# All sixteen row blocks of mm1 by groups of seven products in one of nine tiles, in an order of its own

## The chip, the cores and the metric

The kernel runs on one core of one Trainium2 chip. Its time is device microseconds (us) of one execution of the program; less is better. The engines of the core are called PE (matrix multiplies; its weight loads are PEld), DVE (vector), ACT (activations and copies), POOL (general) and SP (issues transfers). Each engine works through its own queue in order, and semaphores hold an instruction until what it needs is done.

## The reference

Two parts follow each other. First, attention in chunks of 64 tokens: q, k and v have 8 batches, 8 heads, 576 tokens and 64 features, and every chunk attends to itself alone. Then a layer of two matrix multiplies with an exact GELU between them, over 4608 tokens:

```python
scores = scale * np.matmul(q_c, k_c.transpose(0, 1, 2, 4, 3))   # chunks of 64 tokens
attn = softmax(scores)                                          # with 1e-9 in the divisor
x = np.matmul(attn, v_c)                                        # laid out as 4608 x 512
h = x @ w_in                                                    # 512 x 2048
g = 0.5 * h * (1.0 + erf(h * inv_sqrt2))
out = g @ w_out                                                 # 2048 x 512
```

Inputs and the output are float32; the kernel multiplies in bf16 and adds up in float32.

## The kernel before

**Tiles.** The tokens are worked in nine tiles of 512 (NT = 9, index t from 0 to 8): tile t below 8 holds the first 512 tokens of batch t, tile 8 the last 64 tokens of all eight batches. For each tile there is an attention part, which fills x (512 features by 512 tokens, as four slices of 128 partitions), then mm1 (h, 2048 rows by 512 tokens, as sixteen row blocks of 128), then mm2 (the output, 512 by 512). The attention of tile t + 1 and parts of tile t + 2 are laid between the matmuls of tile t.

**mm1, plain.** mm1_slot (L472) makes one row block by four matmuls of 128 x 128 weights (w_in) against 512 columns of x (L477), which add up in one PSUM bank, and one GELU on ACT (L479) that writes h.

**mm1, by seven.** seven_rows (L560) makes four row blocks at once, as a 2 x 2 block matrix of 256 x 256 pieces with seven block products in place of eight. A product is four matmuls of 256 columns (L575). The price is sums: of w_in blocks (w_in_sums, L552, four subtractions or additions on DVE for each group of four row blocks), of x blocks (x_sums, L558, four for each tile, shared by its groups), and of products. The steps of one group, with the names that the orders use (one, two or three primes mark the group: none is row blocks 0 to 3, ' is 4 to 7, '' is 8 to 11):

```python
"p1": product("a", w(0, 0), x_block(t, 0, 0), True)
"s11": AC(place_of("b"), bank["a"])             # ACT copies a to b
"p5": product("d", ws[0], x_sum(1), True), AC(kept, bank["d"])
"p2": product("b", ...)    "c11": gelu of b     # one quarter of h
"p6": product("a", ...)    "s12": d = a + kept  # DVE, L579
"p4": product("d", ...)    "c12": gelu of d
"p7": product("a", ...)    "c22+": kept = a + kept, "c22": gelu of kept
"p3": product("a", w(1, 1), x_sum(4)), gelu of a
```

So a product that adds into bank a (p6, p7, p3) comes after the step that read a before it: p7 after s12, p3 after c22+. PSUM has eight banks in three pools (AT 3, TP 2, MM 3); banks a, b and d of each group are taken from them as they come free.

**Homes.** The sums of w_in for the first group lie in a part of w_out_sb that is not read any more, those of the second in w_in_more, and those of the third in one of the six staging tiles, which third_home (L541) keeps for good at the loads of tile 5; the kept p5 of the third group lies there too.

**The order.** In the tiles 5 to 8 every step is laid by hand in a tuple (FIFTH, LATER, LAST, chosen by WHOLE, L501). A number in it is a plain row block; p, s and c steps are those above; the rest are hooks that whole_hooks (L979) ties to functions. T0 is quad_totals of the next tile (L284: four additions L290, a reciprocal L291, a first spread rc L300, two more reciprocals L296, all on DVE). R0 to R3 are quad_rc (L300, DVE). AV is quad_av (L334, 64 small matmuls on PE). X0 to X3 are quad_x (L341, DVE, they fill x of the next tile). XS1 to XS4 are x_sums of the next tile. S1 to S4, in halves a and b, are g_sum, the sums of h blocks that mm2 needs (L654, L667, DVE). S is quad_S of the tile after the next, with its exponentials on ACT; P0 to P3 are quad_part, its partial sums on DVE (a transpose L256 and a reduction L259 each); KC0 to KC3 are ACT copies for it. exp and gelu load ACT's function table (L865). Each Y is one of the fourteen stations of mm2: two for each of its seven products, 16 matmuls of 256 columns to a product (L731). Y0 opens mm2; what stands before the first Y0 is mm1.

**Tile 7 before.** It follows LATER: three groups by seven (row blocks 0 to 11), the blocks 12 to 15 plain. It has no tile after the next, so S, P and KC do nothing there (tile 8's were made in tile 6); exp and gelu are still issued.

Of the kernel before, what the change touches and what calls it, by code (L numbers as in the profile page):

```python
# [11 lines left out]
def kernel(  # L12
# [26 lines left out]
    NT = B + 1  # L39
# [176 lines left out]
    AT, TP, MM = (ps_at, "at"), (ps_tp, "tp"), (ps_mm, "mm")  # L216
# [255 lines left out]
    def mm1_slot(t, f):  # L472
# [3 lines left out]
        for ks in range(KS):  # L476
# [5 lines left out]
    T0 = 3  # L482
# [14 lines left out]
    LAST = ("p1", "p5", "s11", 13, 14, "p1'", "s11'", "p2", "c11", "p6", "p1''", "s11''", 15, "p5'", "s12", "p7", "p2''", "c22+",  # L497
# [3 lines left out]
    WHOLE = {T0 + 2: FIFTH, NT - 1: LAST, **{t: LATER for t in range(T0 + 3, NT - 1)}}  # L501

    HF = FF // 2
    HD = d_model // 2
# [33 lines left out]
                [w_in_more[:, i] for i in range(4)]]  # L538
    kept_more = []

    def third_home():  # L541

        raw, n = stage_tile(), 4 * HD
        w_in_sum.append([raw[:, i * HD:(i + 1) * HD].bitcast(bf16).rearrange("p (k n) -> p k n", k=2) for i in range(4)])
        kept_more.append(raw[:, n:n + HM * HD].rearrange("p (m n) -> p m n", m=HM))
# [14 lines left out]
    def seven_rows(t, of, pools, kept, bank):  # L560

        h = tiles[t]["h"]
        w, ws = lambda r, c: w_in_block(r, c, of), w_in_sum[of]

        def place_of(to):
            if to not in bank:
                pool, tag = pools[to]
                bank[to] = pool.tile([P, HM, HD], f32, tag=tag, name="hs_ps")
            return bank[to]

        def product(to, left, right, fresh=False):
            hs = place_of(to)
            for f in range(HM):
                for ks in range(2):
                    nc.tensor.matmul(hs[:, f], left[:, ks, f * P:(f + 1) * P], right[:, ks],  # L575
                                     start=(fresh and f == 0 and ks == 0), stop=(ks == 1), skip_group_check=True)

        def plus(to, src):
            nc.vector.tensor_tensor(to, bank[src][:], kept, op=ADD)  # L579

        def gelu(r, c, src):
            n = HM * (2 * of + r)
            nc.scalar.activation(h[:, n:n + HM, HD * c:HD * (c + 1)], src, Act.Gelu)  # L583

        return {
            "p1": lambda: product("a", w(0, 0), x_block(t, 0, 0), True),
            "p5": lambda: (product("d", ws[0], x_sum(1), True), AC(kept, bank["d"][:])),
            "s11": lambda: AC(place_of("b")[:], bank["a"][:]),
            "p2": lambda: product("b", w(0, 1), x_block(t, 1, 0)),
            "c11": lambda: gelu(0, 0, bank["b"][:]),  # L590
            "p6": lambda: product("a", ws[1], x_sum(2)),
            "s12": lambda: plus(bank["d"][:], "a"),
            "p4": lambda: product("d", ws[3], x_block(t, 1, 1)),
            "c12": lambda: gelu(0, 1, bank["d"][:]),
            "p7": lambda: product("a", ws[2], x_sum(3)),
            "c22+": lambda: plus(kept, "a"),
            "c22": lambda: gelu(1, 1, kept),
            "p3": lambda: (product("a", w(1, 1), x_sum(4)), gelu(1, 0, bank["a"][:]))}

    def mm1_seven(t, hooks):  # L600

        if t > 1:
            tiles[t]["h"] = hpool.tile([P, FF, MT], bf16, tag="h", name="h")
        kept = [work.tile([P, HM, HD], f32, tag="t1", name="kept_p5", bufs=2)[:] for _ in range(2 if t in TWICE else 1)]
        bank, more, third = {}, {}, {}
        if t == 1:
            does = seven_rows(t, 1, {"a": TP, "b": AT, "d": AT}, kept[0], bank)
        else:
            does = seven_rows(t, 0, {"a": AT, "b": AT, "d": AT}, kept[0], bank)
        if t in TWICE:  # L610
            does.update((step + "'", do) for step, do in
                        seven_rows(t, 1, {"a": TP, "b": TP, "d": AT}, kept[1], more).items())
            if t not in WHOLE:
                fifth = does["p5'"]
                does["p5'"] = lambda: (more.update(d=bank["b"]), fifth())
        if t in THRICE:
            pools = dict.fromkeys("abd", MM) if t == NT - 1 else {"a": MM, "b": AT, "d": AT}
            does.update((step + "''", do) for step, do in seven_rows(t, 2, pools, kept_more[0], third).items())
        if t in WHOLE:
            order = WHOLE[t][:WHOLE[t].index("Y0")]  # L620
        elif t == T0 + 1:
            order = (4, 5, 6, "p1", "s11", 7, "p2", "p5", "c11", "p6", 8, "s12", "t0", 9, 10, "p4", "p7", "c12", "c22+",
                     "t1", 11, "c22", 12, "p3", "g0", 13, "s3", 14, 15)
        elif t == T0:
            order = ("p1'", "s11'", "x", "p1", "s11", 8, 10, "k", "p6'", "p2", "c11", 11, "p6", "p5", "p5'", "p2'", "c11'", 9, 13,
                     "s12", "p7", "s12'", "p4", "c22+", "p7'", "c12", "c22", "p4'", "c12'", 15, "p3", "c22+'", "p3'", "c22'", 12,
                     "g0", 14)
        elif t == 2:
            order = ("p1", "s11", "p1'", "x", "s11'", 8, "p2", "c11", "p5", 9, "p6", "s12", "p5'", "p6'", "s12'", 10, "p7", 11,
                     "c22+", "c22", "p7'", 12, "p4", "c12", "p3", "c22+'", "p3'", 13, "p4'", "p2'", "k", "c22'", "c11'", "c12'",  # L630
                     "g0", 14, 15, "s3")
        else:
            order = (9, "p1", "s11", 10, 11, "w", "p5", "p2", "c11", "p6", 12, "s12", "w0", "p4", "p7", "c12", "c22+", "w1", 13,
                     "c22", "p3", 14, "g0", "s3", 15)
        for step in order:
            if step in does:
                does[step]()
                continue
            for u in hooks.get(step, ()):
                u()  # L640
            if not isinstance(step, str):
                mm1_slot(t, step)
# [224 lines left out]
    with tc.manual_schedule():  # L867
# [111 lines left out]
        def whole_hooks(t):  # L979

            n = t + 1
            acts = {f"S{i}{'ab'[a]}": lambda i=i, a=a: g_sum(t, i, a) for i in (1, 2, 4) for a in range(2)}
            acts["S3"] = lambda: g_sum(t, 3)
            if n < NT:
                acts.update(T0=lambda: quad_totals(n), AV=lambda: quad_av(n, ALONE),
                            exp=lambda: act_table(Act.Exp), gelu=lambda: act_table(Act.Gelu))
                for m in range(G):
                    acts[f"R{m}"] = lambda m=m: quad_rc(n, m // 2, m % 2)
                    acts[f"X{m}"] = lambda m=m: quad_x(n, m // 2, m % 2)
                    acts[f"XS{m + 1}"] = lambda m=m: x_sums(n, (m,))  # L990
            if n + 1 < NT:
                acts["S"] = lambda: quad_S(n + 1, ALONE)
                for m in range(G):
                    acts[f"KC{m}"] = lambda m=m: k_by_chunk(n + 1, AC, (m,))
                    acts[f"P{m}"] = lambda m=m: quad_part(n + 1, m // 2, m % 2)
            if t == T0 + 2:
                acts.update(W0=lambda: w_in_sums(2, (0, 1)), W1=lambda: w_in_sums(2, (2, 3)))
            e1, e2, slot = {}, {}, 0
            for step in WHOLE[t]:
                if str(step)[0] == "Y":  # L1000
                    slot += 1
                elif step in acts:
                    if slot:
                        e2.setdefault(slot, []).append(acts[step])
                    else:
                        e1[step] = [acts[step]]
            return e1, e2
# [17 lines left out]
        for t in range(1, NT):  # L1025
# [24 lines left out]
            def next_loads():  # L1050
                if t + 3 == NT - 1:
                    load_qk(t + 3, "k")
                    pool_cast_qk(t + 3, "k")
                elif t + 3 < NT:
                    bring_qk(t + 3)
                if n + 1 < NT:
                    load_v_rows(n + 1)
                    cast_v_rows(n + 1, PO)
                if t + 3 == NT - 1:
                    third_home()  # L1060
            if t == T0:
                flip(n + 1, "q")
            elif t > T0:
# [77 lines left out]
```

## Time and profile before

| what | us |
|---|---|
| median of 3 runs | 270.4 (269.82 to 270.89) |
| the profiled execution | 270.2 |
| its span | 268.4, so 1.8 lie around it |
| PE busy | 259.9 (97%) |
| DVE busy | 215.1 (80%) |
| ACT busy | 199.8 (74%) |
| POOL busy | 91.1 (34%) |
| tile 7: mm1 | 214.13 to 226.75, 12.62 |
| tile 7: mm2 | 226.75 to 239.75, 13.00 |
| tile 8: mm1 | 239.75 to 252.37, 12.62 |

The span runs from the first to the last instruction of the profiled execution, and all positions are us from its start. A group line of the profile gives code line, engine, operation, what is written and read, count, busy time and mean duration. A timeline line gives start, duration, engine, code line, operation, what is written and read, shapes and count; idle time of the engine ahead of it and what ended it stand in brackets. A matmul's duration contains its way through the array, so successive matmuls overlap: their rate is read from their starts.

### The profile page before, as it was taken

The page shows a single profiled execution, that of the slowest core. Times are in us where ns is not written, and L with a number is a line of the kernel's source. Part 1 is how long each engine was busy: PE and PEld are TensorE (multiplying, and loading weights), DVE is VectorE, ACT ScalarE, POOL GpSimd, SP SyncE. Part 2 cuts the span into 40 slices and gives each one's busy share as a digit, 9 for nine tenths or more (in the row PEclk, how much of TensorE's full clock was granted, in tenths as well). Part 3 has the DMA queues.
Part 4 walks back from the last instruction along what each step waited for, and adds up shares of the span by engine and source line. Part 5 has one row for each costly group of instructions (what it writes and reads, how often), then busy time and mean ns, then how long its engine had stood idle before and what let it go on. Part 6 is the DMA issues. An engine that isn't in the chain of part 4 may idle for free.

```text
span 268.4 us, 7377 instructions
## 1 busy us (share of the span) xinstructions
PE 259.9 (97%) x2977; PEld 196.7 (73%) x2977; DVE 215.1 (80%) x362; ACT 199.8 (74%) x384; POOL 91.1 (34%) x150
## 2 busy tenths in 40 slices
PE   7699999999999999999999999999999999999994
PEld 2478775556886788678855887688778877887883
DVE  5874877999995899778998999897899979943753
ACT  3767758888676967799977967987899789448810
POOL 7777769511167111912732910305102100000000
PEclk9999999999999999999999999999999999999999
DMA  6999999899699899999899639998954120121014
GB/s 209 265 334 401 391 404 230 230 236 273 217 383 237 192 192 313 235 285 331 220 228 330 156 96 188 220 138 167 272 117 109 42 81 0 42 83 36 1 42 118
DMA packets 104739, 53.97 MB, mean 201 GB/s; under 512 B 72960, under 2 KB 101632, under 8 KB 104704
## 3 DMA queue, kind: packets, MB, share of 16 engines
q1 hardware_dynamic: 104400, 53.23, 75.2%
q8 instruction: 23, 0.38, 0.6%
q10 hardware_dynamic: 304, 0.26, 0.3%
q14 instruction: 12, 0.10, 0.1%
HBM read 36.70 MB, written 9.44 MB: 172 GB/s over the span
## 4 chain that ended last, share of the span: by engine, by line
PE 70%; SPq 11%; DMA 9%; POOL 4%; ACT 3%; issue 1%; DVE 0%; POOLq 0%
PE y_ps L731 26%; PE hs_ps L575 15%; PE h_ps L477 12%; SPq L128 7%; DMA arrival<-in_k_dram 5%; PE h_ps L451 5%; SPq L194 3%; PE y_ps L801 3%; POOL k_nat L164 2%; DMA arrival<-in_v_dram 2%; DMA k_t<-k_nat 2%; ACT k_bd L188 2%; PE h_ps L467 2%; PE y_ps L765 1%; PE av_ps L334 1%
## 5 line engine op out<-in xcount | busy, mean ns | idle before, releaser
L477 PE MATMUL h_ps<-x,w_in_sb 128*128 128x512 bf16 x220 | 53.8, 379 | 0.0
L479 ACT ACTIVATE h<-h_ps 128x512 bf16<-128x512 f32 x69 | 41.2, 600 | 13.1 <-PE h_ps L477 8.6
L731 PEld LDWEIGHTS <-h 128*128 128x128 bf16 x384 | 37.0, 98 | 4.5
L164 POOL CAST q_nat<-arrival 128x512 bf16<-128x512 f32 x31 | 22.2, 755 | 48.4 <-DMA arrival<-in_q_dram 35.2
L477 PEld LDWEIGHTS <-w_in_sb 128*128 128x128 bf16 x220 | 21.5, 98 | 17.8
L583 ACT ACTIVATE h<-hs_ps 128x512 bf16<-128x512 f32 x51 | 29.5, 599 | 4.1 <-PE hs_ps L575 3.9
L731 PE MATMUL y_ps<-v_bd,k_bd 128*128 128x256 bf16 x256 | 29.8, 273 | 0.2
L731 PE MATMUL y_ps<-w_out_sb,h 128*128 128x256 bf16 x256 | 29.7, 273 | 0.0
L214 POOL CAST v_nat<-arrival 128x1024 bf16<-128x1024 f32 x14 | 15.2, 1092 | 42.2 <-DMA arrival<-in_v_dram 24.7
L731 PEld LDWEIGHTS <-k_bd 128*128 128x128 bf16 x256 | 24.7, 98 | 3.7 <-issue 0.5
L164 POOL CAST k_nat<-arrival 128x512 bf16<-128x512 f32 x30 | 20.0, 701 | 16.6 <-DMA arrival<-in_v_dram 11.6
L865 ACT ACT_TABLE_LOAD x18 | 23.1, 1283 | 1.0 <-PEq L1125 0.7
L575 PEld LDWEIGHTS <-w_in_sb 128*128 128x128 bf16 x204 | 20.0, 98 | 5.0 <-issue 0.4
L696 DVE TENSOR_TENSOR kept<-y_ps,kept 128x512 f32<-128x512 f32 (+1 forms) x25 | 16.5, 659 | 7.5 <-issue 3.7
L691 ACT COPY kept<-y_ps 128x512 f32<-128x512 f32 (+1 forms) x26 | 14.4, 557 | 9.4 <-PE y_ps L731 9.1
L575 PE MATMUL hs_ps<-x,w_in_sb 128*128 128x256 bf16 x136 | 19.1, 273 | 0.0
L579 DVE TENSOR_TENSOR hs_ps<-hs_ps,kept_p 128x512 f32<-128x512 f32 x14 | 9.7, 699 | 11.0 <-PE hs_ps L575 7.4
L731 PE MATMUL y_ps<-v_bd,s_sb 128*128 128x256 bf16 x128 | 15.6, 273 | 0.0
L731 PE MATMUL y_ps<-w_out_sb,s 128*128 128x256 bf16 x128 | 15.3, 273 | 0.0
L731 PE MATMUL y_ps<-v_bd,h 128*128 128x256 bf16 x128 | 15.3, 272 | 0.0
L246 ACT ACTIVATE pT<-s_ps 128x512 bf16<-128x512 f32 x28 | 14.4, 600 | 1.2 <-PE s_ps L239 1.1
L451 PE MATMUL h_ps<-x,w_in_sb 128*128 128x256 bf16 x128 | 14.1, 273 | 0.0
(148 smaller groups left out, 522.3 us busy)
## 6 DMA issues: line engine op xcount, KB each, us to landing
arrival<-in_v_dram SPq DMA_DIRECT2D x58, 128.0 KB, 4.1
arrival<-in_q_dram SPq DMA_DIRECT2D x7, 1024.0 KB, 7.1
arrival<-in_k_dram SPq DMA_DIRECT2D x6, 1024.0 KB, 8.4
out_dram<-kept SPq DMA_DIRECT2D x21, 256.0 KB, 2.8
arrival<-in_moe_w_out_dram SPq DMA_DIRECT2D x4, 1024.0 KB, 11.6
arrival<-in_moe_w_in_dram SPq DMA_DIRECT2D x6, 512.0 KB, 8.3
out_dram<-y_sb SPq DMA_DIRECT2D x11, 256.0 KB, 3.0
arrival<-in_k_dram SPq DMA_DIRECT2D x8, 256.0 KB, 5.4
```

The costliest lines, as they stand in the source:

```text
L128: nc.sync.dma_start(to, rows.rearrange("h key d -> key h d"))
L164: copy(st[nm][:, g].rearrange("p j r d -> p r j d"), st[nm + "f"][:, 2 * g:2 * g + 2])
L214: copy(st["v"][:, r::2], st["vf"][:, r::2])
L246: nc.scalar.activation(pT[:].rearrange("p u (c j) -> p u c j", j=J), s_ps[g2][c][:].rearrange("p u (j c) -> p u c j", j=J), Act.Exp, scale ...
L451: nc.tensor.matmul(to[:, cols], left, right[:, cols], start=(start and a == 0), stop=stop, skip_group_check=True)
L477: (nc.tensor.matmul if t else by_halves)(h_ps[:], w_in_sb[:, ks, f * P:(f + 1) * P], tiles[t]["x"][:, ks, :], start=(ks == 0), stop=(ks == ...
L479: nc.scalar.activation(tiles[t]["h"][:, f, :], h_ps[:], Act.Gelu)
L575: nc.tensor.matmul(hs[:, f], left[:, ks, f * P:(f + 1) * P], right[:, ks], start=(fresh and f == 0 and ks == 0), stop=(ks == 1), skip_grou ...
L583: nc.scalar.activation(h[:, n:n + HM, HD * c:HD * (c + 1)], src, Act.Gelu)
L696: nc.vector.tensor_tensor(y_sb[:, ms], ps[:], y_sb[:, ms], op=ADD)
L731: nc.tensor.matmul(to, left(f, m), right[:, f], start=(fresh and (split or m == 0) and f == 0), stop=(f == HF - 1), skip_group_check=True)
L865: nc.scalar.activation(act_scratch[:], rest[:, 0:1], func)
```

## The change

Tile 7 (index NT - 2) gets an order of its own, SEVENTH, and the row blocks 12 to 15 are made by a fourth group of seven products (three primes). For that,

- the fourth group's sums of w_in are made on DVE in mm1 of tile 7 itself, by the new hooks W0 and W1 (two sums each);
- a second staging tile is kept for good, at the loads of tile 6, for these sums and the fourth kept p5 (third_home becomes more_home and is called in the tiles 5 and 6);
- the banks of the third group in tile 7 all come from MM, those of the fourth from MM, AT and MM;
- the four plain blocks 12 to 15 of tile 7 (sixteen matmuls of 512 columns) are gone, and 28 matmuls of 256 columns come in;
- exp and gelu, the two table loads of ACT, do not stand in SEVENTH;
- every other step of tile 7 has a new place. In particular T0 stands after p1', ahead of p2'' and of the first s12; R1 and W0 stand after p4, R2 and AV before the last product p3''', and S1a inside mm1.

The tiles 0 to 6 and the order of tile 8 are untouched.

```diff
+    SEVENTH = ("p1", "s11", "p1''", "s11''", "p5", "p5''", "p2", "c11", "p1'", "T0", "p2''", "p6", "p6''", "c11''", "p5'", "p1'''",
+             "s12", "p7", "s12''", "p4", "R1", "W0", "c22+", "s11'", "p4''", "c12", "p6'", "c12''", "p7''", "s12'", "s11'''",
+             "c22+''", "c22", "p2'", "c11'", "p5'''", "W1", "p6'''", "p7'", "c22''", "p4'", "s12'''", "p2'''", "c12'", "c11'''",
+             "p3", "c22+'", "p3''", "S1a", "c22'", "p7'''", "p3'", "c22+'''", "p4'''", "c22'''", "R2", "AV", "c12'''", "p3'''",
+             "Y0", "R3", "X2", "S1b", "S2a", "S2b", "X0", "X1", "S3", "Y0", "Y1", "X3", "Y1", "S4a", "Y2", "S4b", "Y2", "XS1",
+             "XS3", "Y3", "Y3", "XS2", "Y4", "Y4", "Y5", "XS4", "Y5", "Y6", "Y6")
...
-    WHOLE = {T0 + 2: FIFTH, NT - 1: LAST, **{t: LATER for t in range(T0 + 3, NT - 1)}}
+    WHOLE = {NT - 2: SEVENTH, T0 + 2: FIFTH, NT - 1: LAST, **{t: LATER for t in range(T0 + 3, NT - 2)}}
...
-    def third_home():
+    def more_home():
...
-        bank, more, third = {}, {}, {}
+        bank, more, third, fourth = {}, {}, {}, {}
...
+        if t == NT - 2:
+            does.update((step + "''", do) for step, do in seven_rows(t, 2, dict.fromkeys("abd", MM), kept_more[0], third).items())
+            does.update((step + "'''", do) for step, do in
+                        seven_rows(t, 3, {"a": MM, "b": AT, "d": MM}, kept_more[1], fourth).items())
...
+            if t == NT - 2:
+                acts.update(W0=lambda: w_in_sums(3, (0, 1)), W1=lambda: w_in_sums(3, (2, 3)))
...
-                if t + 3 == NT - 1:
-                    third_home()
+                if t in (T0 + 2, NT - 3):
+                    more_home()
```

(T0 in the code's conditions is the number 3; "T0" in an order is the step of the totals.)

## The prediction

> **What bounds the kernel now.** I read the page first, then who TensorE waited for, then the stretch of tile 7 by engine, then the timelines of PE, DVE and ACT from 213 to 241 us.
>
> ```profile
> PE 259.9 (97%) x2977; PEld 196.7 (73%) x2977; DVE 215.1 (80%) x362; ACT 199.8 (74%) x384; POOL 91.1 (34%) x150
> ...
> PE 70%; SPq 11%; DMA 9%; POOL 4%; ACT 3%; issue 1%; DVE 0%; POOLq 0%
> ```
>
> PE is busy 97% of the span and carries 70% of the chain that ended last. A modelled busy share proves little, so the second view lists PE's waits from 20 us on. It has one row, of 0.2 us:
>
> ```profile
> PE tp L175 <- ACT k_bd L188: 0.2, 1, 0.2
> ```
>
> After 41 us PE never waits. The two stretches of tile 7, mm1 (214.13 to 226.75) and mm2 (to 239.75), with busy times of PE, PEld, DVE, ACT, POOL:
>
> ```profile
> 214.13:226.75 12.62, 12.62 (x102) 9.78 (x100) 11.10 (x22) 10.76 (x21) 0.00 (x0) 1.00 0.13 43
> 226.75:239.75 13.00, 13.00 (x179) 11.50 (x176) 10.75 (x19) 6.15 (x10) 0.00 (x0) 1.00 0.12 42
> ```
>
> In mm1 PE is full, but DVE (11.10 of 12.62) and ACT (10.76) have little room. So the change is paid or earned in PE's matmul rate there, and in any wait that a fuller DVE or ACT gives to PE. All that follows mm1 of tile 7 shifts with it.
>
> **What PE saves.** The rate comes from PE's timeline (start, duration): starts are the measure, as ends overlap.
>
> ```profile
> 216.31 0.60 PE L575 MATMUL hs_ps<-k_bd,w_out_sb 128*128 128x256 bf16 x4
> 216.75 1.89 PE L477 MATMUL h_ps<-x,w_in_sb 128*128 128x512 bf16 x8
> 218.47 0.60 PE L575 MATMUL hs_ps<-x,w_in_sb 128*128 128x256 bf16 x4
> 218.91 0.60 PE L575 MATMUL hs_ps<-k_bd,w_in_more 128*128 128x256 bf16 x4
> ```
>
> Eight matmuls of 512 columns take 218.47 - 216.75 = 1.73 us, 0.2164 each. A product of four matmuls of 256 columns takes 0.4366 us (218.47 to 218.91), 0.109 each. The change removes the plain blocks 12 to 15, 16 x 0.2164 = 3.46 us, and adds seven products, 7 x 0.4366 = 3.06 us: **-0.41 us**, with no setup in it.
>
> One rule would turn this round. The Trainium skill, page "TensorE: Matmul & The Clock Gate", section "Back-to-back issue gap", gives about 131 ns as the sustained spacing of 512-column matmuls with weight loads between. By that figure the sixteen would take about 2.1 us and the edit would cost 0.96 us; this case's row gives 0.2164 us, so the measurement decides for the saving.
>
> **What DVE and ACT get.** ACT gets two more copies (the kept p5''' and s11''') of 0.59 us; its four gelus of 0.60 stay four, as they now end c11''', c12''', c22''', p3'''. DVE gets two more additions (0.69) and four sums of w_in (W0, W1). Those four were made for group 2 in tile 5, into the same kind of home, and have rows:
>
> ```profile
> 163.08 0.41 DVE L552 TENSOR_TENSOR arrival<-w_in_sb 128x512 bf16<-128x512 bf16 x1
> 163.53 0.42 DVE L552 TENSOR_TENSOR arrival<-arrival,w_in_sb 128x512 bf16<-128x512 bf16 x1
> 172.01 0.38 DVE L552 TENSOR_TENSOR arrival<-w_in_sb 128x512 bf16<-128x512 bf16 x1
> 172.31 0.41 DVE L552 TENSOR_TENSOR arrival<-w_in_sb,arrival 128x512 bf16<-128x512 bf16 x1
> ```
>
> I take 0.42. The same line has rows of 0.82 (at 30.6 to 33.3 us) and 1.13 (61.7) while POOL was casting; no POOL instruction runs after 208.9 us, so these are the upper end only. The new home's last casts by POOL are over long before tile 7, so W0 does not wait for them.
>
> **The order is what costs.** DVE still works off tile 6 when tile 7 begins. Its timeline:
>
> ```profile
> 216.12 0.69 DVE L259 TENSOR_REDUCE part<-pt 128x16 f32<-128x512 bf16 x1
> 217.02 0.70 DVE L579 TENSOR_TENSOR hs_ps<-hs_ps,kept_p 128x512 f32<-128x512 f32 x1 [0.22 <-PE hs_ps L575]
> 217.75 0.91 DVE L290 TENSOR_TENSOR total<-part 32x64 f32<-32x64 f32 x4
> 218.69 0.35 DVE L291 RECIPROCAL rb<-total 128x32 f32<-128x32 f32 x1
> 219.08 0.71 DVE L300 STREAM_TRANSPOSE rc<-rb 128x512 f32<-128x512 f32 x1
> 219.80 0.71 DVE L296 RECIPROCAL rb<-total 64x32 f32<-64x32 f32 x2
> ```
>
> The last reduction of tile 6 ends at 216.80. Now s12 (217.02) comes next and T0, the softmax totals of tile 8, after it: 217.75 to 220.51, 2.76 us. In the new order T0 stands ahead of s12. Nothing before it changes, so T0 runs from 216.83 to 219.60 and s12 (0.70) to 220.30. But p7 adds into the bank that s12 reads, so it waits for s12. p7 is the twelfth product: PE is there at 214.13 + 11 x 0.4366 = 218.93. How long PE needs after DVE's end: 0.06 us in the one row where it waited for DVE in the middle of work (q_nat's cast ended at 7.07, PE went on at 7.12), 0.03 where ACT or DVE follow each other. So p7 starts at about 220.34: **a stall of 1.41 us**. Without T0 ahead, s12 could have followed p6 (its fourth matmul ends near 217.8) and been done by 218.5, in time. While p7 waits, everything behind it on PE (sixteen more products, AV, mm2) waits too.
>
> Is there a second wait? I walked the three queues on from there, each instruction at its row's duration (successive DVE starts 0.60 apart for 0.69 us, ACT 0.49 for 0.59), each wait by what it reads or overwrites. The same walk over the old order meets every start of tile 7 within 0.2 us, and all of PE's within 0.1. In the new order PE finds these ready with the margin given: p4'' 0.30 (s12'' ends at 220.90), p5''' 0.46 (c12'' of ACT), p6''' 0.41, p7' 0.30 (s12' ends 223.52), p7''' 0.60, p3' 0.43, p3''' 0.66, the first matmul of mm2 0.34 (a gelu of ACT), the sums S2 1.5, S3 2.0, S4 2.0. So there is no second wait, but DVE runs from 216.8 to 235.8 almost without a pause. The margins exist because PE is already 1.41 late: DVE's work between 216.83 and c22+''' (T0 2.76, eight additions 4.9, R1 0.6, four sums 1.5, S1a 0.6) alone bars p3''' until about 227.3, against 226.6 for a PE that never waits.
>
> AV (0.67 us of PE) moves from inside mm2 to before p3''': same length, nothing gained. R0 to R3, X0 to X3, S1 to S3 and XS1 to XS4 only trade places on DVE; XS4, the last that tile 8 needs, ends at 238.4, 2.3 us ahead. The two table loads that go (1.28 us each at 229.30 and 235.31, with a 0.20 us activation) lie beside mm2, where ACT idles 2.16 and 3.14 us after them: **0**. DMA issues and POOL work do not move; SP keeps its order.
>
> **Sum.** -0.41 + 1.41 = **+1.00 us**. The profiled execution took 270.2 us (span 268.4, 1.8 around it): 271.2. The median of the runs shown is 270.4, which gives 271.4. I say **271.3**.
>
> **Rivals.**
> - No stall, faster: s12 is ready when PE comes. Then only the saving is left, 270.2 - 0.4 = 269.8. It needs DVE 1.4 us earlier than 216.80 at the end of tile 6's reductions; those hang on exponentials that end at 211.68 and are the same in both orders, and DVE's load bars more than half of it anyway. Chance 0.05.
> - A second stall from DVE: the sums of w_in cost 0.82 as in the early rows. It decides from 0.30 us of extra delay on (the margins at p4'' and p7'). W0 brings 0.8, of which 0.5 reaches p7'; W1 brings another 0.8, and p7''' and p3' lose about 0.7 more. +1.2, so 272.4; at 1.13 us for all four, 273.6. Against it: POOL is silent. For it: DVE has no pause to absorb anything. Chance 0.09.
> - The clock falls in the gap. In the trace a gap of 1.13 us (ended at 7.12) was followed by transposes 0.056 us apart, the full rate seen before it, but 1.41 is longer. At the start of the span the first seven 512-column matmuls ran 0.43 us apart, half the rate of 0.2164, for 3.17 us; such a stretch again would lose 1.6 us: 272.8. Chance 0.03. The Trainium skill, "TensorE: Matmul & The Clock Gate", section "Part 1: The HAM clock gate (the "warmup" mystery)", puts the idle window that closes the gate at about 3.4 us; by it this gap does nothing, and no run here shows a gap near that limit.
> - A 512-column matmul is really cheaper than its spacing shows, as by the first rule above. The saving would become a cost: 16 x 0.109 = 1.7 us is a floor for the sixteen if they ran at the rate per instruction of the 256-column ones, so 3.06 - 1.75 = +1.3 and 272.9 with the stall. The trace speaks against it flatly. Chance 0.01.
>
> The forecast keeps 0.82.
>
> **How the numbers follow.** 0.5% is about what a measurement can tell from no change: 1.35 us. The forecast, +1.0, lies 0.35 under that. The runs of before spread from 269.82 to 270.89, so about one comparison in five would pass the bound: 0.16 slower, 0.66 same. The rivals above add 0.13 slower; the stall-free one 0.03 same and 0.02 faster. Slower 0.29, same 0.69, faster 0.02. The range takes the forecast with that spread, 270.3 to 271.9, and reaches up to the second stall: 270.2 to 272.6.
>
> **What would show it.** Right: PE idle once in mm1 of tile 7, at its twelfth product, about 1.4 us, released by DVE's addition (the line of plus); T0's four additions starting at the end of tile 6's last reduction; mm1 with AV taking about 14.3 us; mm2 then about 12.3; spacings of 0.109 us after the gap. Wrong: no such gap, another gap at p4'', p7' or the start of mm2, sums of w_in above 0.5 us, or 256-column spacings above 0.11 us.

## The result, and the profile after

| | before | after |
|---|---|---|
| median of 20 runs, us | 270.72 (269.59 to 272.11) | 271.68 (270.51 to 273.2) |
| ratio, with its 95% interval | | 1.0037 (1.0023 to 1.0051) |
| the profiled execution, us | 270.2, span 268.4 | 272.28, span 270.5 |
| tile 7, from its first product to tile 8's first | 214.13 to 239.75: 25.62 | 215.29 to 241.80: 26.51 |
| of it mm1 | 12.62 | 14.29, with AV in it |
| of it mm2 | 13.00, with AV in it | 12.22 |

The change is slower by 0.96 us by the medians, by 0.89 in tile 7 of the two profiled executions. Their spans differ by 2.1 us: another 1.16 lie ahead of tile 7, where both programs have the same instructions in the same order. Over the profiled executions of this study that stretch took 213.35 to 216.21 us (the longest in e4, which adds work of POOL near its end); the shortest two, 213.35 and 213.69, are of e5 and e6, which share the changed kernel's code up to tile 7, so the 1.16 us are not the change's. So single times can't decide between kernels here, and tile 7's own length is the measure below. What follows tile 7 took 28.7 us in every profile.

Two lines of the page after, first busy time by engine, then the chain that ended last:

```profile
PE 260.6 (96%) x2989; PEld 198.1 (73%) x2989; DVE 216.8 (80%) x368; ACT 197.3 (73%) x382; POOL 90.4 (33%) x150
...
PE 86%; ACT 6%; DVE 3%; DMA 2%; issue 1%; SPq 1%; POOL 0%; DVEq 0%; POOLq 0%
```

They tell little: twelve more matmuls (2977 to 2989), six more DVE instructions, and in PE's share 96% in place of 97%. PE's waits from 20 us on tell it; a row gives the us in total, the times and the longest:

```profile
PE hs_ps L581 <- DVE hs_ps L585: 1.2, 1, 1.2
PE tp L175 <- ACT k_bd L188: 0.2, 1, 0.2
```

One new row: a product (L581) waited once, for a DVE addition (L585, the line of plus, L579 before). Tile 7 by stretch, the busy times again of PE, PEld, DVE, ACT, POOL:

```profile
215.29:229.58 14.29, 13.14 (x179) 11.47 (x177) 13.98 (x30) 11.78 (x24) 0.00 (x0) 1.00 0.11 38
229.58:241.80 12.22, 12.22 (x114) 10.96 (x112) 10.07 (x18) 2.85 (x6) 0.00 (x0) 1.00 0.13 44
```

PE idles 1.15 us in mm1 of tile 7 and not in its mm2; DVE is busy 13.98 of 14.29 us. PE's timeline puts the gap at the twelfth product, p7:

```profile
219.22 0.60 PE L581 MATMUL hs_ps<-k_bd,w_in_more 128*128 128x256 bf16 x4
219.66 0.60 PE L581 MATMUL hs_ps<-x,w_in_sb 128*128 128x256 bf16 x4
221.41 0.60 PE L581 MATMUL hs_ps<-k_bd,w_out_sb 128*128 128x256 bf16 x4 [1.15 <-DVE hs_ps L585]
221.84 0.60 PE L581 MATMUL hs_ps<-x,w_out_sb 128*128 128x256 bf16 x4
```

By starts, p7 was due at 219.66 + 0.44 = 220.10 and came at 221.41: 1.31 us lost (1.15 in the bracket, which counts from the modelled end of the product before). After the gap the products are again 0.43 to 0.44 us apart, so the clock did not fall. DVE in the same time:

```profile
217.29 0.69 DVE L259 TENSOR_REDUCE part<-pt 128x16 f32<-128x512 bf16 x1
218.01 0.91 DVE L290 TENSOR_TENSOR total<-part 32x64 f32<-32x64 f32 x4
218.95 0.35 DVE L291 RECIPROCAL rb<-total 128x32 f32<-128x32 f32 x1
219.34 0.71 DVE L300 STREAM_TRANSPOSE rc<-rb 128x512 f32<-128x512 f32 x1
220.06 0.71 DVE L296 RECIPROCAL rb<-total 64x32 f32<-64x32 f32 x2
220.69 0.67 DVE L585 TENSOR_TENSOR hs_ps<-hs_ps,kept_p 128x512 f32<-128x512 f32 x1
```

The last reduction of tile 6 ends, T0 follows for 2.76 us, and only then s12 (220.69 to 221.36), for which p7 waits.

### The profile page after: what moved, and what is told of

Its sections match the earlier page's. It is cut to its first block, busy times and chain, and to the rows that moved or that the text cites. A ratio compares the mean times of both kernels' runs of the same rounds, so it can differ in the third digit from the quotient of the medians.

```text
span 270.5 us, 7414 instructions
## 1 busy us (share of the span) xinstructions
PE 260.6 (96%) x2989; PEld 198.1 (73%) x2989; DVE 216.8 (80%) x368; ACT 197.3 (73%) x382; POOL 90.4 (33%) x150
## 4 chain that ended last, share of the span: by engine, by line
PE 86%; ACT 6%; DVE 3%; DMA 2%; issue 1%; SPq 1%; POOL 0%; DVEq 0%; POOLq 0%
PE y_ps L741 33%; PE hs_ps L581 20%; PE h_ps L477 15%; PE h_ps L451 5%; PE y_ps L811 3%; DMA arrival<-in_k_dram 2%; PE av_ps L334 2%; ACT k_bd L188 2%; PE h_ps L467 2%; ACT pT L246 1%; PE y_ps L775 1%; DVE k_bd L677 1%; PE s_ps L239 1%; PE y_ps L451 1%; ACT L875 1%
## 5 line engine op out<-in xcount | busy, mean ns | idle before, releaser
L477 PE MATMUL h_ps<-x,w_in_sb 128*128 128x512 bf16 x204 | 49.9, 379 | 0.0
L479 ACT ACTIVATE h<-h_ps 128x512 bf16<-128x512 f32 x65 | 38.8, 600 | 12.9 <-PE h_ps L477 8.4
L164 POOL CAST q_nat<-arrival 128x512 bf16<-128x512 f32 x31 | 19.7, 674 | 48.6 <-DMA arrival<-in_q_dram 30.4
L589 ACT ACTIVATE h<-hs_ps 128x512 bf16<-128x512 f32 x54 | 31.1, 602 | 4.8 <-PE hs_ps L581 4.6
L214 POOL CAST v_nat<-arrival 128x1024 bf16<-128x1024 f32 x14 | 16.0, 1154 | 42.0 <-DMA arrival<-in_v_dram 25.1
L164 POOL CAST k_nat<-arrival 128x512 bf16<-128x512 f32 x30 | 21.0, 733 | 17.9 <-DMA arrival<-in_v_dram 11.7
L581 PEld LDWEIGHTS <-w_in_sb 128*128 128x128 bf16 x216 | 21.0, 98 | 4.9 <-issue 0.4
L701 ACT COPY kept<-y_ps 128x512 f32<-128x512 f32 (+1 forms) x26 | 14.3, 556 | 11.4 <-PE y_ps L741 11.0
L581 PE MATMUL hs_ps<-x,w_in_sb 128*128 128x256 bf16 x144 | 20.1, 273 | 0.0
L585 DVE TENSOR_TENSOR hs_ps<-hs_ps,kept_p 128x512 f32<-128x512 f32 x14 | 9.6, 694 | 11.9 <-PE hs_ps L581 9.0
L581 PEld LDWEIGHTS <-w_out_sb 128*128 128x128 bf16 x112 | 10.9, 98 | 4.5 <-issue 1.3
```

The source lines that it names most:

```text
L164: copy(st[nm][:, g].rearrange("p j r d -> p r j d"), st[nm + "f"][:, 2 * g:2 * g + 2])
L214: copy(st["v"][:, r::2], st["vf"][:, r::2])
L477: (nc.tensor.matmul if t else by_halves)(h_ps[:], w_in_sb[:, ks, f * P:(f + 1) * P], tiles[t]["x"][:, ks, :], start=(ks == 0), stop=(ks == ...
L479: nc.scalar.activation(tiles[t]["h"][:, f, :], h_ps[:], Act.Gelu)
L701: nc.scalar.copy(kept[name][:, ms], ps[:])
```

## The experiments

The theory: T0, whole and ahead of s12 on DVE, is the loss. Rivals: the fourth group gives DVE more than fits, wherever T0 stands; the products cost PE more than their rate; the table loads matter.

**e1, without the totals.** T0 and R0 to R3 of tile 7 are left out; X0 to X3 copy instead of multiply, so tile 8's attention stays undivided.

```diff
-                acts.update(W0=lambda: w_in_sums(3, (0, 1)), W1=lambda: w_in_sums(3, (2, 3)))
+                acts.update(W0=lambda: w_in_sums(3, (0, 1)), W1=lambda: w_in_sums(3, (2, 3)), T0=lambda: None)
+                for m in range(G):
+                    acts[f"R{m}"] = lambda: None
+                    acts[f"X{m}"] = lambda m=m: quad_x_undivided(n, m // 2, m % 2)
```

> The changed kernel without T0 and R0 to R3 of tile 7; X0 to X3 there copy AV's result, so tile 8's attention is left undivided by its sums. Tile 7 (from its first product to tile 8's first) took 25.62 us before and 26.51 after. Theory of the order (T0 ahead of s12 on DVE is the whole loss): no gap of PE at p7, tile 7 at 25.2 us, 0.4 below before, the run about 0.996 to 0.999 of before. Theory that four groups by seven cost PE more than the matmul rate shows: tile 7 stays at 26.2 or more without any gap. Theory that DVE's other work (two more additions, four sums of w_in) stalls PE anyway: a gap of 0.3 us or more later in mm1.

Tile 7 took 25.20 us, 0.42 below before; ratio 1.0004 (0.998 to 1.0029). The mm1 row shows PE without a gap:

```profile
215.51:228.48 12.97, 12.97 (x178) 11.47 (x176) 10.28 (x20) 11.82 (x24) 0.00 (x0) 1.00 0.12 42
```

So 28 products and AV run at full rate (28 x 0.4366 = 12.22, AV 0.67 and its edges), with all eight additions and four sums of w_in in place. The theory that the products cost more falls, and so does that of DVE's other work: mm1 has no later gap either. The run's ratio can't resolve 0.4 us.

**e2, the totals later.**

```diff
-"p1'", "T0", "p2''", ... "s12''", "p4"
+"p1'", "p2''", ... "s12''", "T0", "p4"
```

> The changed kernel with T0 moved from after p1' to after s12'', nothing else. Theory of the order alone: s12 is done by 218.5, p7 does not wait, tile 7 takes 25.2 us. Rival, DVE's load: DVE has no work while it waits for p6, about 1 us, and then T0's 2.76 us stands ahead of c22+, s12' and c22+''; the gap moves to p2' or p6''' or p7' and grows: gaps of about 1.3 and 0.8 us in all 2.1, tile 7 at 27.3 us, 0.8 above the changed kernel and 1.7 above before.

Tile 7 took 27.53 us (27.3 was said), the longest of the study; ratio 1.0122 (1.0057 to 1.0188), by four runs only; tile 7's 1.91 us would make it 1.007. p7 ran at once, and the gap came back as two, larger in sum, in PE's timeline at p5''', where none was expected, and at p7':

```profile
224.62 1.07 PE L581 MATMUL hs_ps<-k_bd,arrival 128*128 128x256 bf16 x8 [1.39 <-DVE arrival L558]
226.28 0.60 PE L581 MATMUL hs_ps<-k_bd,w_in_more 128*128 128x256 bf16 x4 [0.59 <-DVE hs_ps L585]
```

The row of DVE at s12 tells why:

```profile
219.41 0.70 DVE L585 TENSOR_TENSOR hs_ps<-hs_ps,kept_p 128x512 f32<-128x512 f32 x1 [0.79 <-PE hs_ps L581]
```

DVE now idles 0.79 us for p6, and then the 2.76 us of T0 stand ahead of W0 (for which p5''' waits), c22+ and s12' (for which p7' waits). The order alone, in the sense that T0 should come after s12, falls: neither of the two places tried is free for T0 whole, and others were not tried.

**e3, the old kernel with the totals first.** T0 of tile 7 goes ahead of the first s12 in a copy of LATER; three groups and four plain blocks stay.

```diff
-"s11''", 13, "s12", 14, ... "p4", "T0", "c12"
+"s11''", 13, "T0", "s12", 14, ... "p4", "c12"
```

> The kernel before (three groups and four plain blocks in tile 7) with T0 of tile 7 moved ahead of the first s12, nothing else. Theory of the order: PE reaches p7 at 5.2 us after tile 7's start and s12 ends about 6.2 after it: one gap at p7 of 0.9 to 1.0 us, tile 7 at 26.6 us in place of 25.62, as long as in the changed kernel, with no seventh group at all. Rival, the fourth group's load: with only three groups DVE has room, no gap above 0.3 us, tile 7 at 25.6 to 25.9.

Tile 7 took 26.87 us, 1.25 above before, with one gap, at p4; ratio 1.0037 (1.0011 to 1.0062), the same as the change's. (The expectation names p7; in this order p4, of the same group, is the first to need s12.)

```profile
222.04 0.60 PE L581 MATMUL hs_ps<-x,w_out_sb 128*128 128x256 bf16 x4 [1.09 <-DVE hs_ps L585]
```

The place of T0 costs the old kernel a loss of the same kind, without a fourth group. It is 0.27 us more than expected; DVE's last reduction ended 3.03 us after tile 7's start in this run, against 2.68 before and after: 0.35 later, which covers it.

**e4, the sums of w_in on POOL.**

```diff
-nc.vector.tensor_tensor(to[i], a, b, op=op)
+(nc.gpsimd if of == 3 else nc.vector).tensor_tensor(to[i], a, b, op=op)    # W0, W1 ahead of the first s11
```

> The changed kernel with the fourth group's four sums of w_in made by POOL, which is idle there, at the start of tile 7. DVE's queue is 1.6 us shorter, all of it behind s12. Theory of the order: the gap at p7 stays at 1.3 us and tile 7 at 26.5. Rival, DVE's load as a whole: the gap shrinks by 1 us or more, tile 7 at 25.5 or less.

In one execution tile 7 took 27.26 us, with a gap of 1.88 at p7. Neither expected value: POOL had the sums ready ahead of tile 7 (which began at 216.21), but it made them while tile 6's mm2 still ran, from 209.36 to 214.82, and DVE's sums of x ran slowly beside it. POOL, DVE and then PE:

```profile
209.36 1.58 POOL L558 TENSOR_TENSOR arrival<-w_in_sb 128x512 bf16<-128x512 bf16 x1
...
212.20 1.33 POOL L558 TENSOR_TENSOR arrival<-w_in_sb 128x512 bf16<-128x512 bf16 x1
```

```profile
210.03 2.48 DVE L564 TENSOR_TENSOR k_bd<-x 128x512 bf16<-128x512 bf16 x2
212.44 1.37 DVE L564 TENSOR_TENSOR k_bd<-x,k_bd 128x512 bf16<-128x512 bf16 x1
```

```profile
214.46 1.91 PE L741 MATMUL y_ps<-v_bd,h 128*128 128x256 bf16 x16 [1.77 <-DVE kept L706]
```

An x sum took 1.19 to 1.37 us in place of 0.42. PE lost 1.77 us in tile 6 already, waiting for the DVE addition behind these sums, DVE still came to T0 0.7 us later in tile 7, and the gap at p7 grew by as much. As a test of DVE's load it was spoiled, so e5 takes the sums away altogether.

**e5, without the sums of w_in.** The fourth group uses the third's sums.

```diff
-w_in_sum[of]        "R1", "W0", "c22+"  ...  "p5'''", "W1", "p6'''"
+w_in_sum[min(of, 2)]        "R1", "c22+"  ...  "p5'''", "p6'''"
```

> The changed kernel without W0 and W1: the fourth group multiplies with the third group's sums of w_in, so the row blocks 12 to 15 of tile 7 are other numbers; the four sums (1.6 us of DVE) are left out and nothing else runs in their place. Theory of the order: they stand behind s12 and s12'', so the gap at p7 stays at 1.3 us and tile 7 at 26.5. Rival, DVE's load as a whole: the gap shrinks to 0.3 us or less, tile 7 at 25.5.

In one execution tile 7 took 26.51 us, to the hundredth what the change takes, with the same gap; tile 6's last reduction ended 2.68 us after tile 7's start in both:

```profile
219.47 0.60 PE L581 MATMUL hs_ps<-k_bd,w_out_sb 128*128 128x256 bf16 x4 [1.16 <-DVE hs_ps L585]
```

1.6 us of DVE work behind s12 are worth nothing to PE. The rival of DVE's load falls for the change as it stands.

**e6, the totals cut in two.** The four additions stay; reciprocals behind s12'', three of the spreads at the end of mm1, the fourth and S1a just behind the first Y0 (the expectation has these two still in mm1).

```diff
-"T0", ... "s12''", "p4", "R1", ... "c22'''", "R2", "AV"
+"T0", ... "s12''", "T1", "p4", ... "c22'''", "R0", "R1", "R2", "AV"    # T1: the three reciprocals; S1a ahead of S1b
```

> The changed kernel with T0 cut in two: the four additions stay where T0 is, the three reciprocals go behind s12'' and the four spreads with S1a go to the end of mm1, R0 added to them. In the time in which DVE waits for p6 it then has just 0.9 us of work. Theory of order and load together: p7 finds s12 ready, no gap in mm1; the spreads pile up and S2 is late for mm2 by about 0.5 us in two gaps; tile 7 at 25.7, level with before. Theory of the order alone: no gap at all, 25.2. Rival, DVE's load: a gap of 1 us or more stays in mm1, 26.4 or more.

Tile 7 took 25.59 us, 0.11 less than the 25.7 of order and load together: mm1 13.02 without a gap, mm2 12.57 in place of 12.22, with two short delays of PE (0.18 and 0.15 us by starts) where it comes to S2's sums. Ratio 0.9988 (0.9964 to 1.0012). The mm1 row:

```profile
213.69:226.71 13.02, 13.02 (x179) 11.46 (x176) 12.28 (x28) 11.60 (x23) 0.00 (x0) 1.00 0.12 42
```

**e7, cut and laid in order.** The same cut, and a new order of tile 7: additions ahead of s12, reciprocals behind s12'', spreads late in mm1, S1 and S2 first in mm2.

```diff
+"T0", "p2''", "p6''", "c11''", "s12", "s12''", "p5'", "p1'''", "p7", "p4", "p4''", "T1", "s11'", "p2'", "c12", "p6'", "c22+", "W0",
...
+"p3'", "R2", "c22+'''", "R3", "R1", "R0", "p4'''", "c22'''", "c12'''", "AV", "c22'", "p3'''", "Y0", "S1a", "S1b", "S2a", "S2b", "Y0",
...
```

> The cut T0 with an order of tile 7 laid so that every wait has room by the rows' durations: additions ahead of s12, reciprocals behind s12'', spreads late in mm1, S1 and S2 right at the start of mm2 and X0 to X3 behind them; the same work as in the changed kernel. If the loss is nothing but order on DVE: no gap, tile 7 at 25.2 us, 0.4 below before and 1.3 below the changed kernel, so 0.9985 of before. Rival, DVE's load: with 0.1 us of room at some waits, gaps of 0.3 us or more come back, 25.5 or more.

Tile 7 took 25.23 us: 0.39 below before and 1.28 below the change, without a gap. Its DVE rows at the place of the gap:

```profile
218.34 0.91 DVE L290 TENSOR_TENSOR total<-part 32x64 f32<-32x64 f32 x4
219.28 0.70 DVE L591 TENSOR_TENSOR hs_ps<-hs_ps,kept_p 128x512 f32<-128x512 f32 x1
219.88 0.69 DVE L591 TENSOR_TENSOR hs_ps<-hs_ps,arrival 128x512 f32<-128x512 f32 x1
220.60 0.35 DVE L293 RECIPROCAL rb<-total 128x32 f32<-128x32 f32 x1
```

The additions fill the time in which e2 left DVE idle, s12 comes right behind, and the rest of T0 follows later. The ratio of times is 0.9994 (0.9969 to 1.002), not the 0.9985 said: the gain seen in tile 7 of one profile is too small for the times to confirm.

**e8, the old kernel without the table loads.**

```diff
-"KC3", "exp", "X1", ... "Y5", "gelu", "XS4"    # tile 7, in a copy of LATER
+"KC3", "X1", ... "Y5", "XS4"
```

> The kernel before without the two table loads of tile 7, nothing else. My reading: they lie beside mm2 where ACT idles, so nothing: tile 7 at 25.62, ratio 1.000. Rival, they hold ACT's copies and so PE: tile 7 shorter by up to 2.6 us.

Tile 7 took 25.62 us, mm1 12.62 and mm2 13.00 as before; ratio 0.9991 (0.9965 to 1.0017). ACT's busy time in mm2 falls from 6.15 to 3.19 us and PE's length stays.

## Why the prediction was right

- **PE's saving, -0.41.** Right: e1, without the gap, is 0.42 below before. By an estimate from the figure of about 131 ns for 512 columns that the Trainium skill gives ("TensorE: Matmul & The Clock Gate", section "Back-to-back issue gap"), e1 would have been slower than before; the trace does not agree, 0.2164 us held.
- **The stall, +1.41.** Right in place, cause and releaser; 1.31 in size. T0 took 2.76 us as forecast and started 0.03 us behind the reductions. But s12 started at 220.69, before the last reciprocal's row ends (220.77), and took 0.67 in place of 0.70, together 0.11; I had added end to end.
- **No second wait.** Right: one gap. Of the margins, the smallest (0.30 at p4'' and p7') came out at 0.32 and 0.23.
- **AV's move and the table loads, 0.** Right: mm1 with AV 14.29 (forecast 14.3), mm2 12.22 (12.3), and e8 for the loads.
- **The sums of w_in at 0.42.** Right: 0.38 to 0.42. The long rows come back with POOL at work, as in e4 on DVE's sums of x (1.19 to 1.37).
- **The sum, +1.00.** 0.89 in tile 7, 0.96 by the medians; 1.0037 is inside what I called no change a measurement can tell, though with twenty runs it could be told. The median came to 271.68 in place of 271.3; 0.32 of that is the starting value, as the kernel before has 270.72 by twenty runs and 270.4 by three.
- **The order is what costs.** True of the change: e1, e3 and e5 agree. Too short as advice: the text says that without T0 ahead s12 would have been in time, and so it was in e2, but e2 shows that moving T0 there only moves and enlarges the stall. The remark beside it, that DVE's work alone bars p3''' until 227.3, was the better half; the answer was to cut T0 so that a piece fits the idle time and to lay the rest late (e6, e7, with all of T0's work still in tile 7).

The clock rival is out (products 0.44 us apart after the 1.31 us lost). The Trainium skill, "TensorE: Matmul & The Clock Gate", section "Part 1: The HAM clock gate (the "warmup" mystery)", lets the clock fall after an idle window of about 3.4 us. The trace agrees as far as it goes: the gap is shorter, 1.31 us, and the clock stayed.

## What to carry to other kernels

When a matrix engine is full, ask of each added or moved step which instruction on the helper engine it now stands in front of, and who waits for that one: 0.41 us of saved matmuls were spent three times over by one order on the queue of another engine. A long step on such a queue need not be moved whole; cut it, and put the piece that fits into the time in which the engine waits anyway. And where run-to-run spread (here some 2.5 us) hides the effect, compare the length of the touched stretch in the traces.

## What the hardware showed that I had not expected

- In e4 a POOL sum of two bf16 tiles in SBUF (128 x 512) took 1.21 to 1.58 us, and DVE's sums of the same kind, run beside it, took 1.19 to 1.37 us in place of 0.42. A DVE addition that reads PSUM (0.68) and a transpose (0.43) ran beside POOL at their usual length. A cast on POOL does the same: beside POOL's casts of v a 128 x 1024 sum on DVE took 1.52 us in place of 0.69, in e4 and in the changed kernel alike. The Trainium skill, "SBUF — State Buffer", section "Who interferes with whom", says that a DVE instruction with two SBUF inputs contends with a POOL instruction that reads SBUF, for a port pair that only one of them can hold at a time. The trace agrees for DVE's side, by its rows of 1.19 to 1.52 us; what POOL's sums take alone no run here shows.
- How far DVE lags at tile 7's start differs from run to run: tile 6's last reduction ended 2.68 us (before) to 3.03 us (e3) after it, with the same instructions ahead. Where T0 stands ahead of s12, the stall takes its size from that.
